# A decode kernel that streams 119 MB of weights and cache: the first weight load through the plain DMA call, and 16 or 32 equal columns in tail products that had one

## The chip, the cores and the metric

The kernel runs on one core of one Trainium2 chip. The metric is device time of one execution, in microseconds (us). It is quoted as a median over executions. The profile is one execution of the same program under the hardware profiler; its span counts from the first to the last instruction and is 1.7 us shorter than the device time of that run (286.36 us and 284.7 us for the kernel before). All executions count as fast (none lies over 1.5% above the fastest of its kernel).

## The reference, cut to what matters

One token (one row of 640 numbers) passes through attention over a cached window of 4096 keys per head, then through a gated MLP.

```python
x = A_x                                            # [1, 1, 640]
# attention: 32 heads of 192, the last W = 4096 positions of the caches
q = (layernorm(x) @ wq)                            # wq [640, 6144]
p = softmax(q . k_cache[:, :, -W:, :] * 192**-0.5)
h = x + (p @ v_cache[:, :, -W:, :]) @ wo           # wo [6144, 640]
# gated MLP on one position; S = 1, so w_sp and b_sp are single numbers
z  = gelu(layernorm(h) @ w_in)                     # w_in [640, 1536]
z1, z2 = z[:768], layernorm(z[768:])
out = h + (z1 * (w_sp * z2 + b_sp)) @ w_out        # w_out [768, 640]
```

All tensors are bf16. Keys and values are 50 MB each, wq and wo 7.9 MB each, w_in and w_out 2.9 MB together. Each is read once.

## The kernel before: the parts that matter

All large loads are issued by SyncE on one DMA queue, in the order of use: wq, then keys and values of 16 pairs of heads with wo between them, then the last wo piece, w_in and w_out. A load is issued when a buffer is free. The helper `load` builds the DMA instruction by hand instead of calling `nc.sync.dma_start`.

```python
def load(out, in_):
    eng = nc.sync
    eng.add_instruction(mybir.InstDMACopy(
        name=nc.get_next_instruction_name(), mode="Copy", queue="qSPDynamicHW",
        ins=eng.lower_ap_dma(in_, for_custom_bir_dma=True),
        outs=eng.lower_ap_dma(out, for_custom_bir_dma=True)))

wq_v = A_wq.rearrange("(c p i) n -> c p (i n)", c=DC, i=4)   # per c: 32 rows of 48 KB

def dma_wq(i):
    t = kvp.tile([P, KVE], BF16, tag="kv", name="wq_t")
    for c in range(2 * i, min(2 * i + 2, DC)):
        load(t[:, (c % 2) * HD:(c % 2 + 1) * HD], wq_v[c])
    tiles[("wq", i)] = t
```

The tail starts with the last products of probabilities and values. The attention output `o` of the last four heads goes through wo as 30 products with the weights stationary and one moving column; the partial row sums of the earlier heads are folded in first.

```python
# project(), last q only
for i in range(RQ):                                # RQ = 6
    for nb in range(DC):                           # DC = 5
        nc.tensor.matmul(attn_ps[:, nb:nb + 1], lhsT=wo_t[:, i * D + nb * P:i * D + (nb + 1) * P],
                         rhs=o[:, i:i + 1], start=False, stop=...)
...                                                # h, its sums, LayerNorm (cut)
def half_in(f0):
    zv = bank()
    for c in range(DC):
        for fb in range(FHC):                      # FHC = 6: 30 products a call
            nc.tensor.matmul(zv[:, fb:fb + 1], lhsT=w_in_sb[:, c, f0 + fb * P:f0 + (fb + 1) * P],
                             rhs=hb1[:, c:c + 1], start=..., stop=...)
    return zv[:, 0:FHC]

z2_ps = half_in(Fh)                                # gelu, second LayerNorm (cut)
z1_ps = half_in(0)                                 # gelu, gate (cut)
for c in range(FHC):
    for g in range(NG):                            # NG = 4, one group of columns of the array each
        nc.tensor.matmul(orow[32 * g:32 * g + 1, :], lhsT=gv[:, c:c + 1],
                         rhs=w_out_sb[:, c, g * OW:(g + 1) * OW], start=False, stop=(c == FHC - 1))
```

## Time and profile before

| | before |
|---|---|
| median of the first 3 executions | 286.6 us (286.29 to 286.65) |
| first weight packet starts | 2.07 us |
| 16 or more weight and cache packets in flight | 265.0 us |
| last w_out packet ends | 280.95 us |
| granted TensorE clock, mean | 0.803 |

The rows on packets are read from the trace's packet records.

The page of the kernel before. PE stands for TensorE's products, PEld for its weight loads, DVE for VectorE, ACT for ScalarE and POOL for GpSimd. In each row of digits a digit is a slice of 1/40 of the span in tenths; PEclk is the granted TensorE clock (the share of full clock that a throttle lets the engine have), DMA the mean busy share of the 16 engines.

```profile
span 284.7 us, 3101 instructions
PE 167.1 (59%) x1110; PEld 65.3 (23%) x1110; DVE 218.4 (77%) x288; ACT 75.2 (26%) x380; POOL 2.3 (1%) x10
...
PEclk9999979796598557955799558955797797999785
DMA  8999999999998999999999999999999999999993
GB/s 332 435 435 408 435 429 402 444 463 435 435 435 382 435 442 443 427 464 424 414 442 421 443 428 439 407 457 428 410 435 456 442 442 383 435 435 425 401 406 141
```

The DMA engines are the resource that is busy from end to end. VectorE comes next, at 77% of the span and 91% between 36 and 214 us, and the DMA engines stay busy there too (431 GB/s). The Trainium skill, "DMA: Bandwidth & Descriptors", section "Where 436 GB/s comes from", puts the ceiling of the core's SBUF ports at 435 GB/s; many slices here read 435 (some more, because a packet is booked whole at its start), and the mean is 420. So the kernel is within 4% of that ceiling, and, as far as this goes, only what lies before the first packet and after the last landings can go.

Busy time in two short stretches at the start of the kernel before. The columns are the stretch, its length, the busy time of PE, PEld, DVE, ACT and POOL, the granted clock, the DMA share and GB/s. A packet is booked whole at its start, so the DMA share can exceed 1.

```profile
1.60:2.00 0.40, 0.00 (x0) 0.00 (x0) 0.12 (x1) 0.40 (x1) 0.40 (x2) 1.00 0.01 3
2.00:2.40 0.40, 0.19 (x5) 0.19 (x5) 0.37 (x4) 0.22 (x2) 0.40 (x1) 1.00 4.25 1352
```

Nothing but the 1.2 KB of x moves before 2.0 us.

The tail on the timeline of the kernel before. Columns: start, duration, engine, line, operation, tile, and in brackets the idle time before it with what ended it.

```profile
273.26 0.51 PE L478 MATMUL attn_ps<-o_1888,wo_t 128*128 128x1 bf16 x15 [0.32 <-DVE o_1888 L464]
274.08 0.53 PE L478 MATMUL attn_ps<-o_1888,wo_t 128*128 128x1 bf16 x15 [0.30 <-DMA wo_t<-in_A_wo_dram]
...
274.96 0.48 PE L578 MATMUL sm_ps<-sums_1922,avgD_f 128*128 128x1 f32 x2 [0.36 <-DVE h_pc L574]
...
275.78 1.22 PE L589 MATMUL sm_ps<-hb_1930,w_in_sb 128*128 128x1 bf16 x30
...
279.16 0.96 PE L589 MATMUL sm_ps<-hb_1930,w_in_sb 128*128 128x1 bf16 x30
...
280.51 0.17 DVE L623 TENSOR_TENSOR gv<-z_2038,gz 128x6 bf16<-128x6 f32 x1
...
280.73 0.97 PE L626 MATMUL sc_ps<-w_out_sb,gv 128*1 128x160 bf16 x24 [0.61 <-DVE gv L623]
```

The second half of the last wo products waited for its weights. In the chain of work that ended last (start, length, what), that DMA is the link before the tail:

```profile
260.22 13.82 DMA wo_t<-in_A_wo_dram
...
274.08 0.54 PE attn_ps L478 x15
```

Busy time by stretch of the kernel before, columns as above. Read the third number from the right, the granted clock.

```profile
264.00:268.00 4.00, 3.59 (x38) 1.61 (x39) 0.61 (x4) 2.20 (x4) 0.00 (x0) 0.61 0.93 396
268.00:272.00 4.00, 3.44 (x92) 2.44 (x86) 2.89 (x4) 0.48 (x1) 0.00 (x0) 0.97 0.99 400
272.00:276.00 4.00, 2.62 (x59) 2.27 (x56) 0.98 (x6) 0.51 (x3) 0.00 (x0) 0.89 1.05 400
276.00:280.00 4.00, 3.51 (x75) 2.83 (x72) 2.49 (x14) 1.01 (x4) 0.00 (x0) 0.50 0.96 372
```

The clock record has two values only, 1.0 and 0.5, which agrees with the Trainium skill, "TensorE: Matmul & The Clock Gate", section "Part 1: The HAM clock gate", which says that the ratio is binary. It falls to 0.5 at 275.10 us and stays there to the end.

### The profile page before, as it was taken

How to read it: one execution, taken by the hardware profiler on the slowest of the kernel's cores; microseconds unless marked ns; L12 is line 12 of the kernel's file. 1: busy time of each engine (PE TensorE's matmuls, PEld its weight loads, DVE VectorE, ACT ScalarE, POOL GpSimd, SP SyncE). 2: the span in 40 equal slices, each digit the busy share in tenths (PEclk: the TensorE clock that was granted, in tenths of full speed). 3: DMA queues.
4: the chain of work that ended last, by engine and by line, in shares of the span. 5: the costliest groups of instructions: out<-in, count | busy, mean ns of one | idle time of the engine just before them, and what ended most of it. 6: DMA issues, size and time to landing. Idle time of an engine off the chain costs nothing.

```text
span 284.7 us, 3101 instructions
## 1 busy us (share of the span) xinstructions
PE 167.1 (59%) x1110; PEld 65.3 (23%) x1110; DVE 218.4 (77%) x288; ACT 75.2 (26%) x380; POOL 2.3 (1%) x10
## 2 busy tenths in 40 slices
PE   0329935773755377725852585536971767764774
PEld 0103412221211022211220121112320222321463
DVE  7300099889999999998499999996699949995443
ACT  2001247413274431122344440143101010202301
POOL 3000000000000000000000000000000000000000
PEclk9999979796598557955799558955797797999785
DMA  8999999999998999999999999999999999999993
GB/s 332 435 435 408 435 429 402 444 463 435 435 435 382 435 442 443 427 464 424 414 442 421 443 428 439 407 457 428 410 435 456 442 442 383 435 435 425 401 406 141
DMA packets 5404, 119.53 MB, mean 420 GB/s; under 512 B 973, under 2 KB 2254, under 8 KB 2830
## 3 DMA queue, kind: packets, MB, share of 16 engines
q1 hardware_dynamic: 5384, 119.35, 97.8%
q8 instruction: 8, 0.13, 0.2%
q14 instruction: 6, 0.05, 0.0%
q10 hardware_dynamic: 6, 0.00, 0.0%
HBM read 119.34 MB, written 0.00 MB: 419 GB/s over the span
## 4 chain that ended last, share of the span: by engine, by line
DMA 42%; DVE 41%; PE 13%; issue 2%; SPq 1%; ACT 0%; DVEq 0%; ACTq 0%
DVE k_t L316 22%; DMA k_t<-in_A_k_cache_dram 21%; DMA v_t<-in_A_v_cache_dram 9%; DMA wq_t<-in_A_wq_dram 7%; DMA wo_t<-in_A_wo_dram 5%; PE sc_ps L264 5%; DVE S L309 5%; DVE ob L437 4%; DVE S L330 4%; PE sc_ps L323 3%; PE pv_174 L412 1%; PE attn_ps L473 1%; SPq L58 1%; PE sm_ps L340 1%; DVE gm L342 1%
## 5 line engine op out<-in xcount | busy, mean ns | idle before, releaser
L316 DVE TENSOR_TENSOR k_t<-k_t,q_205 128x6144 bf16<-128x6144 bf16 x32 | 107.1, 3351 | 13.1 <-DMA k_t<-in_A_k_cache_dram 13.1
L323 PE MATMUL sc_ps<-k_t,ident_bf 128*128 128x512 bf16 x282 | 87.1, 468 | 50.6 <-DVE k_t L316 50.6
L306 ACT ACTIVATE k_t<-k_t 128x192 bf16<-128x192 bf16 x144 | 49.9, 347 | 32.8 <-DVE k_t L316 32.8
L323 PEld LDWEIGHTS <-ident_bf 128*128 128x128 bf16 x282 | 30.6, 113 | 98.3 <-issue 63.9
L306 ACT ACTIVATION_READ_ACCUMULATOR k_t<-k_t 128x1 f32 x144 | 26.8, 186 | 0.0
L309 DVE TENSOR_REDUCE S<-k_t 128x16 f32<-128x3072 bf16 x8 | 26.8, 3345 | 0.0
L264 PE MATMUL sc_ps<-wq_t,xn_126 128*128 128x512 bf16 x60 | 17.4, 449 | 10.4 <-DMA wq_t<-in_A_wq_dram 8.1
L330 DVE TENSOR_REDUCE S<-sc_ps 128x16 f32<-128x512 f32 (+1 forms) x32 | 21.8, 682 | 0.5 <-PE sc_ps L323 0.5
L273 DVE TENSOR_SCALAR sp_f<-sm_ps 128x1 f32<-128x1 f32 x3 | 0.3, 153 | 25.3 <-PE sm_ps L270 25.3
L359 ACT ACTIVATE E_125<-S,bias 128x64 bf16<-128x64 f32 x10 | 3.5, 360 | 48.1 <-DVE bias L349 48.1
L359 ACT ACTIVATE E_123<-S,bias 128x64 bf16<-128x64 f32 x12 | 4.2, 360 | 41.9 <-DVE bias L349 41.9
L359 ACT ACTIVATE E_124<-S,bias 128x64 bf16<-128x64 f32 x10 | 3.5, 361 | 37.9 <-DVE bias L349 37.9
L266 ACT ACTIVATE q_205<-sc_ps 128x512 bf16<-128x512 f32 x6 | 3.6, 597 | 30.1 <-PE sc_ps L264 30.1
L264 PEld LDWEIGHTS <-xn_126 128*128 128x128 bf16 x60 | 6.5, 109 | 20.9 <-issue 13.6
L412 PE MATMUL pv_174<-v_t,E_124 128*8 128x512 bf16 (+1 forms) x72 | 8.9, 521 | 2.0 <-DMA v_t<-in_A_v_cache_dram 2.0
L342 DVE TENSOR_REDUCE gm<-sm_ps 2x1 f32<-2x128 f32 x16 | 4.5, 278 | 7.1 <-PE sm_ps L340 7.1
L412 PE MATMUL pv_172<-v_t,E_125 128*8 128x512 bf16 (+1 forms) x72 | 7.5, 472 | 3.1 <-DMA v_t<-in_A_v_cache_dram 3.1
L412 PE MATMUL pv_174<-v_t,E_123 128*8 128x512 bf16 (+1 forms) x48 | 5.8, 521 | 1.0 <-DMA v_t<-in_A_v_cache_dram 1.0
L412 PE MATMUL pv_172<-v_t,E_123 128*8 128x512 bf16 (+1 forms) x72 | 6.2, 424 | 0.0
L412 PE MATMUL pv_174<-v_t,E_125 128*8 128x512 bf16 (+1 forms) x48 | 5.0, 474 | 1.6 <-DMA v_t<-in_A_v_cache_dram 1.6
L412 PEld LDWEIGHTS <-E_125 128*8 128x8 bf16 (+1 forms) x120 | 3.5, 87 | 9.3 <-issue 7.2
L412 PEld LDWEIGHTS <-E_124 128*8 128x8 bf16 (+1 forms) x120 | 3.6, 89 | 8.3 <-issue 6.4
(237 smaller groups left out, 148.3 us busy)
## 6 DMA issues: line engine op xcount, KB each, us to landing
k_t<-in_A_k_cache_dram SPq DMA_DIRECT2D x15, 3072.0 KB, 29.8
v_t<-in_A_v_cache_dram SPq DMA_DIRECT2D x15, 3072.0 KB, 29.6
wq_t<-in_A_wq_dram SPq DMA_DIRECT2D x5, 1536.0 KB, 11.2
wo_t<-in_A_wo_dram SPq DMA_DIRECT2D x7, 960.0 KB, 19.9
k_t<-in_A_k_cache_dram SPq DMA_DIRECT2D x2, 1536.0 KB
v_t<-in_A_v_cache_dram SPq DMA_DIRECT2D x1, 1536.0 KB
w_in_sb<-in_B_w_in_dram SPq DMA_DIRECT2D x2, 576.0 KB, 14.6
wo_t<-in_A_wo_dram SPq DMA_DIRECT2D x2, 480.0 KB, 13.8
```

What stands on the lines that cost most here:

```text
L58: eng.add_instruction(mybir.InstDMACopy(name=nc.get_next_instruction_name(), mode="Copy", queue="qSPDynamicHW", ins=eng.lower_ap_dma(in_, ...
L264: nc.tensor.matmul(psv, lhsT=xn2[:, c, a, :], rhs=wc[:, gq:gq + 4, a, w0:w0 + P], start=(c == 0 and a == 0), stop=(c == DC - 1 and a == 1))
L266: nc.scalar.activation(out=q2f[:, gq:gq + 4, w0:w0 + P], in_=psv, func=ACT.Copy, scale=scale / 16)
L306: nc.scalar.activation(out=k3[:, j, :], in_=k3[:, j, :], func=ACT.Copy, accum_out=S[:, j:j + 1])
L309: nc.vector.tensor_reduce(out=st[t]["S"][:, J - JS:J], in_=products(t)[:, J - JS:J, :], axis=AX.X, op=ALU.add)
L316: nc.vector.tensor_tensor(out=kc, in0=kc, in1=q2[:, t:t + 1, :].to_broadcast([P, JC, Dh]), op=ALU.mult)
L323: nc.tensor.matmul(psv, lhsT=ident_bf[:], rhs=products(t)[:, j0:j1, n * g:(n + 1) * g], start=(n == 0), stop=(n == Dh // g - 1))
L330: nc.vector.tensor_reduce(out=S[:, j0:j1], in_=st[t]["ps"][ch], axis=AX.X, op=ALU.add)
L342: nc.vector.tensor_reduce(out=gm[:], in_=mT[0:2, 0:P], axis=AX.X, op=ALU.max)
L359: nc.scalar.activation(out=E[:, :, a], in_=S[:], func=ACT.Exp, bias=bias[:, a:a + 1], accum_out=zq[q][:, a, b:b + 1])
L412: nc.tensor.matmul(pv[p0:p0 + 2 * n, :].rearrange("p (k r i) -> p k r i", k=n, r=32), lhsT=E[:, j0:j0 + n, :].rearrange("p j a -> p (j a)" ...
L437: nc.vector.tensor_reduce(out=ob[:, i0:i0 + ni], in_=flat.rearrange("p (k r i) -> p i r k", k=n, i=ni), axis=AX.X, op=ALU.add)
```

## The change

Two independent parts. The first issues the first wq load with the plain call `nc.sync.dma_start` and gives it rows of 12 KB instead of 48 KB. The second streams 16 equal columns through the last wo products (a power of two that still fits beside the row sums in the bank), and 32 through the w_in products; the readers take column 0. The results are the same numbers. Its likely purpose is to keep TensorE busier at no cost.

```diff
     def dma_wq(i):
         t = kvp.tile([P, KVE], BF16, tag="kv", name="wq_t")
         for c in range(2 * i, min(2 * i + 2, DC)):
-            load(t[:, (c % 2) * HD:(c % 2 + 1) * HD], wq_v[c])
+            dst = t[:, (c % 2) * HD:(c % 2 + 1) * HD]
+            if c == 0:
+                nc.sync.dma_start(out=dst, in_=A_wq[0:P])
+            else:
+                load(dst, wq_v[c])
 ...
-    rows = attn_ps[:, DC + 3:DC + 3 + CUT[1]]
+    AW = 16
+    attn = attn_ps[:, 0:(DC + 1) * AW].rearrange("p (c w) -> p c w", w=AW)
+    rows = attn_ps[:, (DC + 1) * AW:(DC + 1) * AW + CUT[1]]
 ...
-                    nc.tensor.matmul(attn_ps[:, nb:nb + 1], lhsT=wo_t[...],
-                                     rhs=o[:, i:i + 1], start=False,
+                    nc.tensor.matmul(attn[:, nb, :], lhsT=wo_t[...],
+                                     rhs=o[:, i:i + 1].to_broadcast([P, AW]), start=False,
 ...                                 # fold(): 2 x 16 columns likewise
+    ZW = 32
     def half_in(f0):
-        zv = bank()
+        zv = bank()[:, 0:FHC * ZW].rearrange("p (f w) -> p f w", w=ZW)
 ...
-                nc.tensor.matmul(zv[:, fb:fb + 1], lhsT=w_in_sb[...], rhs=hb1[:, c:c + 1],
+                nc.tensor.matmul(zv[:, fb, :], lhsT=w_in_sb[...],
+                                 rhs=hb1[:, c:c + 1].to_broadcast([P, ZW]),
 ...
-        return zv[:, 0:FHC]
+        return zv[:, :, 0]
```

No load and no product is added or moved.

More of the change, by code (lines that the diff above doesn't have):

```diff
@@ L276 @@
     CUT = (0, 3 * P, D)
-    rows = attn_ps[:, DC + 3:DC + 3 + CUT[1]]
+    AW = 16
+    attn = attn_ps[:, 0:(DC + 1) * AW].rearrange("p (c w) -> p c w", w=AW)
+    rows = attn_ps[:, (DC + 1) * AW:(DC + 1) * AW + CUT[1]]
     nc.vector.memset(rows, 0.0)
-    nc.vector.memset(attn_ps[:, DC:DC + 1], (eps * DC) ** 0.5)
+    nc.vector.memset(attn[:, DC, :], (eps * DC) ** 0.5)
     obq = {}
@@ L477, in project @@
                 for nb in range(DC):
-                    nc.tensor.matmul(attn_ps[:, nb:nb + 1], lhsT=wo_t[:, i * D + nb * P:i * D + (nb + 1) * P],
-                                     rhs=o[:, i:i + 1], start=False,
+                    nc.tensor.matmul(attn[:, nb, :], lhsT=wo_t[:, i * D + nb * P:i * D + (nb + 1) * P],
+                                     rhs=o[:, i:i + 1].to_broadcast([P, AW]), start=False,
                                      stop=(q == NQ - 1 and i == RQ - 1 and nb == DC - 1))
@@ L486, in fold @@
             w = 2 if c + n < DC else 1
-            nc.tensor.matmul(attn_ps[:, c:c + n * (w - 1) + 1:n], lhsT=rows_sb[:, c * P:(c + 1) * P], rhs=halfsel[:, 0:w],
+            nc.tensor.matmul(attn[:, c:c + n * (w - 1) + 1:n, :], lhsT=rows_sb[:, c * P:(c + 1) * P], rhs=halfsel[:, 0:w, None].to_broadcast([P, w, AW]),
                              start=(c == 0), stop=False)
@@ L573 @@
     sums2 = [const.tile([P, 1], F32, name=f"sums2{k_}") for k_ in range(2)]
-    nc.vector.tensor_scalar(out=h_pc[:], in0=attn_ps[:, 0:DC], scalar1=1.0, scalar2=0.0, op0=ALU.mult, op1=ALU.add,
+    nc.vector.tensor_scalar(out=h_pc[:], in0=attn[:, 0:DC, 0], scalar1=1.0, scalar2=0.0, op0=ALU.mult, op1=ALU.add,
                             accum_out=sums2[0][:])
-    nc.scalar.activation(out=hsq[:], in_=attn_ps[:, 0:DC + 1], func=ACT.Square, accum_out=sums2[1][:])
+    nc.scalar.activation(out=hsq[:], in_=attn[:, :, 0], func=ACT.Square, accum_out=sums2[1][:])
     mean_ps = bank()[:, 0:1]
@@ L583 @@
     rstd2 = ln_rstd16(neg_var(mean_ps, square_ps))
+    ZW = 32
     def half_in(f0):
-        zv = bank()
+        zv = bank()[:, 0:FHC * ZW].rearrange("p (f w) -> p f w", w=ZW)
         for c in range(DC):
             for fb in range(FHC):
-                nc.tensor.matmul(zv[:, fb:fb + 1], lhsT=w_in_sb[:, c, f0 + fb * P:f0 + (fb + 1) * P], rhs=hb1[:, c:c + 1],
+                nc.tensor.matmul(zv[:, fb, :], lhsT=w_in_sb[:, c, f0 + fb * P:f0 + (fb + 1) * P],
+                                 rhs=hb1[:, c:c + 1].to_broadcast([P, ZW]),
                                  start=(c == 0 and fb == 0), stop=(c == DC - 1 and fb == FHC - 1))
-        return zv[:, 0:FHC]
+        return zv[:, :, 0]
     z2_ps = half_in(Fh)
```

## The prediction

> **What bounds the kernel now.** The DMA stream, end to end. The page's DMA row stands at 9 from the second slice to the last but one, 119.5 MB at a mean of 420 GB/s over a span of 284.7 us. The packet records show all 16 DMA engines busy at once for 255.6 us and never fewer than ten between 2.7 us, soon after the first weight packet (2.07 us), and 279.6 us; the last w_out packet ends at 280.95 us. VectorE (77%) and TensorE (59%) have slack. So only two pieces can shrink: the 2.07 us before the stream, and the tail after the last weights.
>
> **The tail** (timeline, from 274 us). The last wo half lands at 274.08; 15 products; LayerNorm sums; 30 w_in products (18 from 275.78, the other 12 held by their DMA until 276.53); gelu at 277.39, released by VectorE's rstd chain, not by the products; 30 more products 279.16 to 280.12; VectorE's gz ends 280.40, level with gelu z1 at 280.42; w_out products 280.73 to about 281.7; store; end.
>
> **What the change does.**
> 1. First wq load. SyncE issues it at 0.74 us and takes 0.55 us; its first packet starts 0.78 us later. The change gives it the plain call that the x and spatial loads use: their later ScalarE issues took 0.22 and 0.27 us (the first 0.50). Estimate: 0.2 to 0.3 us saved, and as the DMA engines never go idle, all later landings move earlier by about that. Against it: 12 KB rows for 48 KB. A 12 KB packet takes 461 ns, a 48 KB one 1815, so 8 against 2 cost 58 ns per engine. Net estimate: 0.2 us.
> 2. 16 columns (wo). One-column pairs are spaced 25 ns at full clock. The Trainium skill, "TensorE: Matmul & The Clock Gate", section "Back-to-back issue gap", gives 1 to 64 columns one floor, about 25 ns; the trace agrees at one column. 16 columns should be free.
> 3. 32 columns (w_in). These run at granted clock 0.5 (from 275.45 us), spaced 26 to 27 ns. 512-column products at full clock follow every 213 ns with their weight load hidden, so a 32-column stream (estimate 26.7 ns at half clock, by scaling) should also hide it. Cost: about 26 ns more for the last of each 30.
> 4. Strided PSUM reads, wider memset, wider fold: under 20 ns on the path.
>
> The likely purpose of 2 and 3 is to show the clock throttle a busier TensorE. If full clock came back in the tail, the w_out products (133 ns apart per group of four at half clock) and the LayerNorm matmuls would save an estimated 0.3 to 0.5 us. I doubt it: before each return to 1.0 the trace has a window of nearly unbroken 512-column work, and 30 x 32 columns fill only 0.8 of 3.4 us.
>
> **Sum.** Minus 0.2 us (load), plus 0.05 us (columns), minus 0.1 us for the chance of a better clock: 286.35 us, 80% range 285.7 to 286.9. Chances: faster by over 2% 0.01, within 2% 0.98, slower 0.01.
>
> **What would show it.** First issue at or under 0.35 us and first packet by 1.85 us; last w_out packet and wo landing earlier by about 0.2 us; wo spacing 25 ns; w_in spacing 26 to 28 ns; granted clock still 0.5 from about 275 us; time from wo landing to the end unchanged within 0.1 us.
>
> **What would make it wrong.** If weight loads do not overlap short moving streams, w_in spacing becomes about 53 ns and the second 30 cost 0.8 us on the path. If the throttle stays open, up to 0.5 us is won, of which the last w_out landing caps part. If the first load's latency, not its issue, sets the first packet, step 1 gives nothing.

Three slips in it: the clock fell at 275.10 us in the profile's time, not at 275.45. Its 255.6 us is the time with exactly 16 large packets in flight; 16 or more were in flight for 265.0 us. And the 512-column products at full clock mostly follow every 215 to 216 ns, not 213. None of them changes its argument.

## The result, and the profile after

The changed kernel takes 286.14 us (median of 6, 286.11 to 286.40) beside 286.55 us for the kernel before (median of 6 executions). The ratio is 0.9987, with a 95% interval of 0.9974 to 1.0000. Ratios here are the mean time of one kernel's fast runs over that of the other's from the same rounds, so they are not quite the ratio of the quoted medians. The prediction of 286.35 us, range 285.7 to 286.9, holds.

| | before | after | difference |
|---|---|---|---|
| first issue of SyncE | 0.55 us | 0.38 us | -0.17 |
| first weight packet starts | 2.07 us | 1.75 us | -0.32 |
| last packet of the last wo piece ends | 273.68 us | 273.32 us | -0.36 |
| h starts on VectorE | 274.74 us | 274.42 us | -0.32 |
| its LayerNorm result hb starts | 275.49 us | 275.27 us | -0.22 |
| gate product gv starts | 280.51 us | 280.28 us | -0.23 |
| last w_out packet ends | 280.95 us | 280.59 us | -0.36 |
| span | 284.66 us | 284.45 us | -0.21 |

The page after:

```profile
span 284.5 us, 3101 instructions
PE 170.5 (60%) x1110; PEld 66.5 (23%) x1110; DVE 218.3 (77%) x288; ACT 75.2 (26%) x380; POOL 2.3 (1%) x10
...
PEclk9999996889599757995687557957896679979575
DMA  8999999999998999999999999999999999999993
```

The start of the changed kernel, stretches as before:

```profile
1.60:2.00 0.40, 0.00 (x0) 0.00 (x0) 0.12 (x1) 0.40 (x1) 0.40 (x2) 1.00 1.65 276
2.00:2.40 0.40, 0.00 (x0) 0.00 (x0) 0.36 (x4) 0.22 (x2) 0.40 (x1) 1.00 0.00 0
```

Nine engines now start before 2.0 us; in between none starts, and the other seven start by 2.65 us (before: eleven by 2.32 and five by 2.90). The tail on the timeline after:

```profile
273.23 1.05 PE L484 MATMUL attn_ps<-o_1888,wo_t 128*128 128x16 bf16 x30 [0.32 <-DVE o_1888 L470]
...
274.64 0.59 PE L584 MATMUL sm_ps<-sums_1922,avgD_f 128*128 128x1 f32 x2 [0.36 <-DVE h_pc L580]
...
275.56 1.07 PE L597 MATMUL sm_ps<-hb_1930,w_in_sb 128*128 128x32 bf16 x30
...
278.94 0.98 PE L597 MATMUL sm_ps<-hb_1930,w_in_sb 128*128 128x32 bf16 x30
...
280.28 0.17 DVE L632 TENSOR_TENSOR gv<-z_2038,gz 128x6 bf16<-128x6 f32 x1
...
280.50 0.97 PE L635 MATMUL sc_ps<-w_out_sb,gv 128*1 128x160 bf16 x24 [0.59 <-DVE gv L632]
```

There are two readings. The second thirty of w_in take 0.98 us with 32 columns and took 0.96 us with one: the columns are free, as forecast. And the first float32 product for the LayerNorm (L584, before L578) takes 0.59 us where it took 0.48: the 0.32 us won at the start has become 0.22 by then. The cause is the clock:

```profile
264.00:268.00 4.00, 3.96 (x38) 1.68 (x39) 0.51 (x3) 1.99 (x4) 0.00 (x0) 0.50 0.96 408
268.00:272.00 4.00, 4.00 (x92) 2.70 (x86) 2.92 (x4) 0.48 (x1) 0.00 (x0) 0.76 0.98 399
272.00:276.00 4.00, 2.91 (x65) 2.65 (x64) 1.18 (x6) 0.51 (x3) 0.00 (x0) 0.67 1.05 400
276.00:280.00 4.00, 3.40 (x68) 2.64 (x64) 2.39 (x14) 1.06 (x5) 0.00 (x0) 0.50 0.93 362
```

In this execution the clock fell at 273.36 us, before those products, and in the kernel before at 275.10, after them. The same skill section says that the activity window runs free of the program. The traces agree: within each profile all changes of the clock lie whole multiples of about 3.41 us apart (here 252.88, 256.30, 263.12, 269.95 and 273.36 us), and the place of this grid differs from execution to execution. Over the profiles without fillers (below) and with an unshifted start, the last fall lies anywhere from 273.36 to 276.58 us. load_only with one column and all_wq with 16 and 32, whose grids happen to lie within 0.06 us of each other, have the same last fall (274.65 and 274.71 us). So this 0.1 us is most likely a draw of one execution and not a cost of the change.

The clock was also at 0.5 from 263.12 to 269.95 us, through most of the last value products. In the profile after, the view of the chain that ended last therefore names TensorE's value products instead of the wo DMA.

```profile
234.08 29.92 DMA v_t<-in_A_v_cache_dram
...
264.04 1.87 PE pv_172 L418 x12
...
269.15 1.54 PE pv_174 L408 x29
...
273.23 1.06 PE attn_ps L484 x30
```

This view leaves out short waits, and here that misleads. The wo products started at 273.23 us, at nearly the same time as before. But the first of the second fifteen started at 273.72 us, 0.05 us after its weights' landing (273.67 us by the semaphore record) and 0.11 us after the product before it, where the first fifteen follow each other every 25 to 30 ns. In the kernel before it started at 274.08 us, also 0.05 us after the landing (274.03), and 0.46 us after the product before it. So the wo load was still last in both. Its 0.36 us came through, less the 0.04 us by which the second fifteen were slower at half clock: h starts 0.32 us earlier. What shrank is the wait for it, from 0.44 to 0.09 us. In after_again (below) nothing was left of it: the second fifteen followed after 29 ns.

That the two are so close was not in the prediction at all. At the end of the stream the DMA and the TensorE chain of the last value products arrive nearly together, and the clock decides which is last.

### The profile page after: what moved, and what is told of

Its sections match the earlier page's. It is cut to its first block, busy times and chain, and to the rows that moved or that the text cites. A ratio compares the mean times of both kernels' runs of the same rounds, so it can differ in the third digit from the quotient of the medians.

```text
span 284.5 us, 3101 instructions
## 1 busy us (share of the span) xinstructions
PE 170.5 (60%) x1110; PEld 66.5 (23%) x1110; DVE 218.3 (77%) x288; ACT 75.2 (26%) x380; POOL 2.3 (1%) x10
## 4 chain that ended last, share of the span: by engine, by line
DVE 38%; DMA 37%; PE 21%; issue 2%; SPq 1%; ACT 0%; DVEq 0%; ACTq 0%
DMA k_t<-in_A_k_cache_dram 20%; DVE k_t L322 20%; DMA v_t<-in_A_v_cache_dram 11%; PE sc_ps L329 8%; DMA wq_t<-in_A_wq_dram 6%; PE sc_ps L268 5%; DVE S L315 5%; DVE ob L443 4%; DVE S L336 3%; PE attn_ps L479 2%; PE pv_172 L418 1%; PE sm_ps L346 1%; PE pv_174 L418 1%; DVE gm L348 1%; SPq L58 1%
## 5 line engine op out<-in xcount | busy, mean ns | idle before, releaser
L329 PE MATMUL sc_ps<-k_t,ident_bf 128*128 128x512 bf16 x282 | 89.2, 477 | 48.0 <-DVE k_t L322 48.0
L268 PE MATMUL sc_ps<-wq_t,xn_126 128*128 128x512 bf16 x60 | 18.3, 469 | 10.1 <-DMA wq_t<-in_A_wq_dram 7.9
```

The costliest lines, as they stand in the source:

```text
L268: nc.tensor.matmul(psv, lhsT=xn2[:, c, a, :], rhs=wc[:, gq:gq + 4, a, w0:w0 + P], start=(c == 0 and a == 0), stop=(c == DC - 1 and a == 1))
L329: nc.tensor.matmul(psv, lhsT=ident_bf[:], rhs=products(t)[:, j0:j1, n * g:(n + 1) * g], start=(n == 0), stop=(n == Dh // g - 1))
```

## The experiments

Theory A: the gain is the earlier start of the weight stream, passed through whole, since the DMA engines never run dry; the columns do nothing. Rivals: B, the columns give it, through the products or the clock; and within A, that the smaller rows and not the issue path start the engines earlier. Each call ran on one chip and shares 11 executions of the kernel before; its median differs by up to 0.4 us from call to call, so compare within a call. An execution over 287 us of a kernel that mostly stays under it is called a stray below. All twelve runs gave correct results.

### First call: one part at a time, the row form, and a late start

**load_only**: the kernel before with the first-load hunk of the diff alone.

> Only the first wq load is changed (plain call, 12 KB rows); the tail products keep one column. Theory A (the gain is the earlier start of the weight stream, passed through whole): ratio to before about 0.9987, first weight packet at about 1.75 us, last w_out packet end near 280.6 us, time about 0.3 to 0.4 us under before. Theory B (the wider columns give the gain, through the clock or the products): ratio 1.000. Theory C (both give half): about 0.9993.

Measured: 286.18 us (285.95 to 286.35, 5 runs), before 286.48 us (11 runs). Ratio 0.9984, interval 0.9967 to 1.0001. First issue 0.39 us, first weight packet at 1.75 us:

```profile
1.60:2.00 0.40, 0.00 (x0) 0.00 (x0) 0.12 (x1) 0.40 (x1) 0.40 (x2) 1.00 1.13 246
```

The load alone gives the whole 0.30 us in the median. The last w_out packet ended at 280.79 us where 280.6 was expected; the landing of the last packets differs by 0.2 us from run to run.

**cols_only** and **cols_again**: the changed kernel with the first-load hunk undone. Run twice.

```diff
-            dst = t[:, (c % 2) * HD:(c % 2 + 1) * HD]
-            if c == 0:
-                nc.sync.dma_start(out=dst, in_=A_wq[0:P])
-            else:
-                load(dst, wq_v[c])
+            load(t[:, (c % 2) * HD:(c % 2 + 1) * HD], wq_v[c])
```

> Only the 16 and 32 columns; the first wq load is as before. Theory A: ratio 1.000 (up to 0.05 us slower), first weight packet at about 2.07 us, w_in products still 26 to 27 ns apart, granted clock 0.5 from some point between 272 and 276 us to the end. Theory B: ratio about 0.9987. Theory C: 0.9993.

Measured: 287.16 us (286.37 to 288.32, 6 runs), ratio 1.0018, interval 0.9994 to 1.0041. Three of the six lie at 286.37, 286.41 and 286.85, the other three at 287.48 to 288.32. One of the eleven executions of the kernel before on that chip was such a stray too (287.89). First packet as before the change:

```profile
1.60:2.00 0.40, 0.00 (x0) 0.00 (x0) 0.12 (x1) 0.40 (x1) 0.40 (x2) 1.00 0.01 3
```

This is no gain, but the three strays left it open whether the columns harm. So it was run again, beside the changed kernel, in the second call.

> The same kernel as cols_only, again, because three of its six times lay over 287 us against one of eleven of the kernel before. If the wider columns do harm: again several times over 287, ratio about 1.002. If those were stray executions (of the kind that the kernel before also shows once, at 287.89): median 286.4 to 286.6, ratio 1.000 within 0.0005.

Measured in the second call: 286.80 us (286.64 to 286.85, 6 runs, no stray), before 286.74 us. Ratio 0.9989, interval 0.9971 to 1.0007; it is under 1 only because four of the eleven executions of the kernel before were strays (287.45 to 288.25). Without those four the kernel before has a median of 286.67 us, 0.13 under this one. So the columns neither gain nor, in these twelve executions, do harm that repeats. A cost of about 0.1 us is not excluded.

**rows_only**: one column, the first load issued by hand as before, but with rows of 12 KB.

```diff
-            load(t[:, (c % 2) * HD:(c % 2 + 1) * HD], wq_v[c])
+            dst = t[:, (c % 2) * HD:(c % 2 + 1) * HD]
+            load(dst, A_wq[0:P] if c == 0 else wq_v[c])
```

> One column, and the first wq load in 12 KB rows but issued the old way. It parts the row form from the issue path. Theory A1 (the shorter issue starts the stream earlier): issue 0.55 us, first packet at 2.0 to 2.1 us, ratio 1.000 to 1.0002. Theory A2 (the smaller rows start the engines earlier, whatever the issue path): first packet before 1.9 us, ratio about 0.9987.

Measured: 286.60 us (286.41 to 286.96, 5 runs), ratio 0.9998, interval 0.9979 to 1.0018. The issue took 0.58 us and the first packet started at 2.09 us. The row form alone starts nothing earlier; the issue path does. (The plain call with 48 KB rows was not tried.) It also shows that the path does more than shorten the issue: the plain call's first packet starts 0.64 us after the end of its issue (1.11 to 1.75 us), the hand-built one's 0.78 us after (1.29 to 2.07).

This run bears on another point by the way: what a faster clock in the tail is worth. Here the clock stayed open until 276.58 us, and gv started at 280.37 us, 0.14 us earlier than in the kernel before. Yet the w_out products ended at 281.70 us as there, because they took 1.11 us instead of 0.97:

```profile
280.59 1.11 PE L630 MATMUL sc_ps<-w_out_sb,gv 128*1 128x160 bf16 x24 [0.61 <-DVE gv L627]
```

In the instruction records the last group of four started 0.32 us after the one before it instead of 0.13, and 0.04 us after the landing of the last w_out load (281.36 us by the semaphore record). So the last landing caps what a faster tail can win. From that landing to VectorE's reading of the products it took 0.45 us in the kernel before (281.30 to 281.75) and 0.59 us in the changed kernel (280.94 to 281.53). With the clock fully open (warm_tail, below) it took 0.33 us. So full clock in the tail was worth some 0.12 us before and 0.25 us after the change, by estimate from these three profiles.

**late_start**: the changed kernel with four small loads ahead of the first weight load.

```diff
+    junk = const.tile([1, 4, 64], BF16)
+    for k_ in range(4):
+        nc.sync.dma_start(out=junk[:, k_, :], in_=A_x[0, :, 64 * k_:64 * k_ + 64])
+
     def dma_wq(i):
```

> The changed kernel with four small loads of x (128 bytes each, into a scratch that nobody reads) issued on SyncE ahead of the first wq load; each should take about 0.25 to 0.35 us of issue. Theory A: the first weight packet moves by 1.0 to 1.4 us against the changed kernel and the time follows one to one, so about 287.1 to 287.5 us, ratio to before 1.002 to 1.0035. Rival (a late start is made up somewhere in 280 us of stream, since VectorE and buffers set part of the pace): under half of the shift arrives, ratio under 1.001.

Measured: 287.68 us (287.53 to 288.59, 5 runs), ratio 1.0041, interval 1.0022 to 1.0061: slower, with the interval clear of 1. The first weight packet started at 2.94 us, 1.19 us later than in the changed kernel, and the last w_out packet ended at 281.86 us, 1.27 us later. Against load_only on the same chip, which has one column, the median rose by 1.50 us. So a shift of the start arrives at the end at least in full. About 0.3 us more than the shift is left open: the columns differ, the four loads also use up completion semaphores, and the issue of the third wq load took 1.00 us against 0.93.

### Second call: repeat, double the columns, hold the clock

**after_again**: the changed kernel once more.

> The changed kernel beside cols_again on one chip. Theory A (earlier start): 0.3 to 0.4 us under before, ratio 0.9986, and lower than cols_again by the same. If the columns harm: no gain over before.

Measured: 286.50 us (286.48 to 287.98, 6 runs, one stray), ratio 0.9988, interval 0.9965 to 1.0011. The median is 0.30 us under cols_again, which differs by the first load alone, and 0.24 under before (0.17 without the four strays of before). The size of the gain, 0.2 to 0.4 us, repeats on each chip where it was tried; each single ratio has an interval that just reaches 1.

**cols64**: the suspected cost of the columns, doubled.

```diff
-    ZW = 32
+    ZW = 64
```

> The changed kernel with 64 instead of 32 equal columns in the w_in products: the suspected cost doubled. At granted clock 0.5 the products should follow each other every 53 ns instead of 26 to 27 ns (64 columns at 1.2 per ns), so the second thirty takes 1.6 us instead of 0.8. That thirty is level with VectorE's gz chain, so the time should rise by 0.6 to 0.8 us, to about 286.9. It would show that 32 columns were free because the stream is just as long as the weight load beneath it. Rival (the floor is per instruction, and 64 columns are also free): spacing under 30 ns, time unchanged. If the granted clock returns to 1.0 in the tail through the added columns, spacing 27 ns and the time falls.

Measured: 287.37 us (286.75 to 288.22, 6 runs), ratio 1.0014, interval 0.9991 to 1.0037; 0.87 us over after_again in the median, where 0.6 to 0.8 was expected. Products follow each other every 53 to 54 ns. The timeline has the two thirties:

```profile
275.78 1.76 PE L597 MATMUL sm_ps<-hb,w_in_sb 128*128 128x64 bf16 x30
...
279.35 1.78 PE L597 MATMUL sm_ps<-hb,w_in_sb 128*128 128x64 bf16 x30
```

1.78 us where 32 columns took 0.98: 32 columns were free at the 0.5 clock only because their stream (32 columns at 1.2 per ns, 26.7 ns; 512-column products follow every 427 ns at this clock) is no longer than the 26 to 27 ns that one column already took. The Trainium skill, "TensorE: Matmul & The Clock Gate", section "Back-to-back issue gap", lists 1 to 64 columns as one cost at full clock; at the 0.5 clock the trace does not allow that reading, and the same section's cold formula (columns over 1.2 per ns) gives the 53 ns that were measured. The granted clock in the tail stayed at 0.5 even with 64 columns.

**warm_tail**: seven products of 512 columns that nobody reads, where TensorE waits in the tail, into a PSUM bank that is free by then.

```diff
+    def filler(bank_, n):
+        for _ in range(n):
+            nc.tensor.matmul(bank_[:], lhsT=ident_bf[:], rhs=q2[:].rearrange("p a b -> p (a b)")[:, 0:512],
+                             start=True, stop=True)
 ...
     values(NP - 1, vt, LAST[-2], J)
+    filler(pv_tiles[0], 1)
     scaled(NP - 1)
     columns(oT, NQ - 1, 1)
+    filler(pv_tiles[0], 1)
     project(NQ - 1, oT)              # and one filler between its two halves
+    filler(pv_tiles[0], 1)
 ...
     h_rows(0, NG // 2)
+    filler(pv_tiles[0], 1)
 ...
     z1_ps = half_in(0)
+    filler(pv_tiles[0], 2)
```

> The changed kernel with seven products of 512 columns that nobody reads, put where TensorE waits in the last 12 us (one after the last value products, one before and one in the middle of and one after the last wo products, one before the second LayerNorm's sums, two after the last w_in products). It asks whether the throttle can be held open in the tail and what that is worth. If the activity suffices: granted clock 1.0 to the end, w_out groups 67 ns apart instead of 133, time 0.2 to 0.4 us under the changed kernel. If not: the fillers run at 427 ns each and delay the chain, clock 0.5 as before, time 0.1 to 0.5 us over the changed kernel. I think the second the likelier.

Measured: 286.31 us (285.99 to 286.56, 6 runs, no stray), ratio 0.9973, interval 0.9952 to 0.9993, and 0.19 us under after_again in the median. The likelier-seeming outcome was wrong: in the profiled execution the clock stayed open from 271.20 us to the end. The grid of its clock changes lies within 0.1 us of those of load_only, cols64 and all_wq, whose clocks fell at 274.65 to 274.71 us, so the grid's place is not what kept it open. But the work also came later there (see below), so one profile does not put it down to the fillers alone.

```profile
272.00:276.00 4.00, 3.46 (x80) 2.47 (x81) 0.69 (x5) 0.51 (x3) 0.00 (x0) 1.00 1.05 399
276.00:280.00 4.00, 3.15 (x81) 2.70 (x83) 2.63 (x15) 1.02 (x5) 0.00 (x0) 1.00 0.96 372
```

From the first wo product to the start of the last w_out product it took 7.41 us, against 7.90 in the changed kernel's profile and 8.10 before. The timeline has where it came from, and what caps it:

```profile
275.54 0.38 PE L594 MATMUL sm_ps<-sums,avgD_f 128*128 128x1 f32 x2
...
280.87 0.83 PE L647 MATMUL sc_ps<-w_out_sb,gv 128*1 128x160 bf16 x24 [0.47 <-DVE gv L644]
```

The LayerNorm product takes 0.38 us instead of 0.59. The w_out groups of four follow each other every 68 to 70 ns instead of 133, but the last group started only 0.32 us after the one before it: it needs the last landing of the stream (281.42 us, as in rows_only). In this execution the value stage had been cold as well (0.55 in 264 to 268 us, 0.60 in 268 to 272) and the first wo product started at 274.06 us, 0.83 us later than in the profile after.

### Third call: are the columns worth something then, and where do the strays come from

**warm_onecol**: warm_tail with one column.

```diff
-    AW = 16
+    AW = 1
 ...
-    ZW = 32
+    ZW = 1
```

> warm_tail with the wide columns taken back to one (the fillers and the early load stay). It asks whether the columns do anything for the clock once there is other work: in warm_tail the 60 w_in products of 32 columns are some 1900 of the columns streamed after 275 us. If they matter: the clock falls to 0.5 again somewhere from 274 to 279 us (w_in products 26 to 27 ns apart in the second thirty, w_out groups 120 to 133 ns), time 0.1 to 0.3 us over warm_tail. If the fillers alone do it: clock 1.0 to the end, time as warm_tail within 0.1 us.

Measured: 286.74 us (286.15 to 287.67, 6 runs, three of them at 287.00 or over), ratio 0.9984, interval 0.9958 to 1.0010. In the profile the clock fell to 0.5 at 275.56 us and stayed there. That is what was expected if the columns matter, but the window in which it fell began 1 us later than the one in warm_tail, and the run was a stray, so one profile each does not settle it. What the columns do for the clock stays open.

The stray is of use for itself. Busy time and chain of this execution, 287.67 us:

```profile
264.00:268.00 4.00, 2.97 (x34) 1.49 (x35) 1.98 (x5) 2.19 (x4) 0.00 (x0) 0.67 0.90 386
268.00:272.00 4.00, 4.00 (x67) 2.51 (x59) 2.92 (x4) 0.48 (x1) 0.00 (x0) 0.50 1.00 405
```

```profile
269.40 2.12 PE pv L408 x25
271.53 1.07 PE attn_ps L495 x6
...
274.37 0.51 PE attn_ps L486 x15
```

TensorE was busy for the whole of 268 to 272 us at the 0.5 clock, and the wo products started at 274.37 us (0.32 us of it a filler), where they started at 273.26 and 273.23 us in the profiles before and after. The weights had long landed (last packet 273.56 us). The one other profile of an execution well above its kernel's others, late_start's 288.59 us (the other four at 287.53 to 287.73), has no filler and shows the same: clock 0.50 in 268 to 272 us, and the first wo product 1.02 us after the last wo packet (275.61 and 274.59 us), where the changed kernel's profile has it 0.09 us ahead of that packet. A cold start of the stage is not enough: after_again and cols_again were at 0.5 from 263.8 to 270.7 us and took 286.52 and 286.85 us. In the two strays the half clock lasted to 272.15 and 273.55 us.

**warm_both**: warm_tail and six more fillers near 262 us, where TensorE waited some 2 us for value data.

```diff
     scaled(NP - 3)
     vt = tiles.pop(("v", NP - 2))
+    filler(pv_tiles[1], 6)
     values(NP - 2, vt, 0, J // 2)
```

> warm_tail with six more unread products of 512 columns where TensorE waits some 2 us for value data near 262 us. The idea under test: executions 1 to 1.7 us over the rest (4 of 11 of the kernel before in the last call, at mean clocks of 0.78 to 0.81) are those in which the clock stays at 0.5 through the last value products, so that they end after the wo data has landed. If so: the clock is at 1.0 from before 268 us on, no execution over 287, and a spread of under 0.5 us, median as warm_tail or 0.1 to 0.2 us lower. If the stray executions come from elsewhere (the DMA, say), they stay.

Measured: 286.72 us (286.62 to 286.88, 6 runs), ratio 0.9983, interval 0.9959 to 1.0008. No stray, where five of the eleven executions of the kernel before on that chip were strays (287.57 to 288.30). The value stage is now warm:

```profile
264.00:268.00 4.00, 3.80 (x62) 1.86 (x63) 2.31 (x6) 2.21 (x5) 0.00 (x0) 1.00 0.94 400
268.00:272.00 4.00, 2.58 (x80) 2.00 (x70) 2.41 (x5) 0.47 (x1) 0.00 (x0) 1.00 0.99 403
272.00:276.00 4.00, 3.69 (x56) 2.66 (x57) 0.88 (x6) 0.51 (x3) 0.00 (x0) 0.50 1.05 401
```

But now TensorE waited from 268.6 us for the last value pieces, and the clock fell at 272.02 us; the tail was cold, the median no better than the good executions of before (286.71 us without the strays).

**all_wq**: all five wq loads as plain calls in 12 KB rows, beside the changed kernel's columns.

```diff
-            dst = ...
-            if c == 0:
-                nc.sync.dma_start(out=dst, in_=A_wq[0:P])
-            else:
-                load(dst, wq_v[c])
+            nc.sync.dma_start(out=t[:, (c % 2) * HD:(c % 2 + 1) * HD], in_=A_wq[c * P:(c + 1) * P])
```

> The changed kernel with all five wq loads as plain calls in 12 KB rows. Theory A says that only the first issue lies on the path, since the DMA engines are never idle after it; the other four only cost 58 ns per engine and load (8 packets of 460 ns against 2 of 1815): last w_out packet 0.1 to 0.3 us later than in the changed kernel, time 0.1 to 0.3 us over it, so 0.1 to 0.2 us under before. Rival (each shorter issue gains): another 0.2 us or more under the changed kernel.

Measured: 286.99 us (286.26 to 287.95, 6 runs, two strays), ratio 0.9994, interval 0.9967 to 1.0021. The later issues took 0.41 to 0.68 us instead of 0.54 to 0.93, and nothing came of it; the last w_out packet ended at 281.01 us, 0.18 and 0.27 later than in the two other profiles of the call with one plain load (280.83 and 280.74). That is the size of the expected packet cost, but the time itself is too noisy to say more than that there is no further gain.

### Fourth call: both gaps filled

**warm_more**: warm_both with three more fillers at the wait near 268.6 us.

```diff
-    values(NP - 1, vt, 0, LAST[-3])
+    values(NP - 1, vt, 0, LAST[1])
+    filler(pv_tiles[0], 3)
+    values(NP - 1, vt, LAST[1], LAST[-3])
```

> warm_both with three more unread 512-column products in the 1.3 us for which TensorE waited near 268.6 us for the last value pieces, since the clock there fell to 0.5 at 272.0 us. The hope: clock 1.0 from about 264 us to the end, no execution over 287, and 0.4 to 0.7 us under the median of before (ratio 0.997 to 0.9985 in its fast runs, lower where before has strays). If the fillers come late (after a cold stretch they take 427 ns each), the last value products are delayed and it is no better than warm_tail, about 0.3 us under before.

Measured: 286.32 us (286.25 to 286.61, 6 runs), before 286.82 us (11 runs, four at 287.34 to 288.09). Ratio 0.9974, interval 0.9954 to 0.9994. No stray again. The clock fell later than in warm_both, at 274.35 us, not "never":

```profile
268.00:272.00 4.00, 3.53 (x86) 2.37 (x85) 1.83 (x3) 0.00 (x0) 0.00 (x0) 1.00 0.97 396
272.00:276.00 4.00, 3.88 (x60) 2.46 (x58) 0.94 (x6) 0.50 (x3) 0.00 (x0) 0.79 1.05 400
```

With warm_tail this is the best version found: both beat the kernel before with an interval clear of 1, by 0.26 to 0.27%. In the means warm_more gains some 0.7 us; the early start, about 0.3 us, is less than half of it, and the strays of the kernel before (four of eleven, each about 1 us long) are of the size of the rest, by estimate from these numbers.

## Why the prediction was right, point by point

- **The stream bounds the kernel and a shift of its start arrives whole: right.** In the profiles -0.32 us at the first packet became -0.36 at the last. late_start moved the start by 1.19 us and the time by at least as much.
- **The load term was mis-sized: -0.2 us net predicted, about -0.3 measured** (load_only -0.30 in the median; the changed kernel -0.41, and -0.24 on another chip). The estimate took its 0.2 to 0.3 us from ScalarE's tiny issues of 0.22 and 0.27 us; the issue of a 1.5 MB load fell by only 0.17 us, to 0.38, over the 0.35 forecast. What was missed is that the wait from the end of the issue to the first packet fell as well, by 0.14 us (0.78 to 0.64). rows_only shows that both belong to the path, not to the rows. The predicted packet cost of 0.06 us is too small for these runs to see.
- **Free columns: right.** Spacing 26 to 27 ns in the w_in products as predicted. The wo products kept 25 ns for the six that started before the clock fell, and 26 to 27 after. cols_again and cols64 agree with the reason given. The 0.05 us set aside for their cost is not resolved.
- **The throttle stays shut for the changed kernel: right,** at 0.5 from 273.36 us on, and so the 0.1 us credited for the chance of a better clock did not come. Nor was there as much to win: the prediction put full clock in the tail at 0.3 to 0.5 us, of which the last w_out landing would cap part. By the landing times (see rows_only) it caps more than was thought, leaving by estimate 0.12 us in the kernel before and 0.25 us in the changed one. The reason given, that a full window of dense work is needed, is too strict for staying open: warm_tail held the clock through 274.61 to 278.03 us with 58 products and 2,356 moving columns.
- **Tail unchanged within 0.1 us: missed by little.** From the last wo packet to the end of the span it took 11.13 us after and 10.98 before; the clock's earlier fall explains nearly all of the difference (0.04 us in the second fifteen wo products, 0.10 us in the LayerNorm products).
- **What was not foreseen:** the last value products are nearly as late as the stream, and their clock decides about 1 us of single executions. In the last four calls 14 of 44 executions of the kernel before are strays over 287 us, at a mean clock of 0.786; the other 30 have 0.806. Fillers in the wait before that stage removed them (0 of 12 in warm_both and warm_more, 9 of 22 of the kernel before in the same calls). That a value stage cold to its end makes the strays is supported by this and by the two that were profiled, and not proven: the unprofiled ones have no clock record by time, and warm_tail and cols_again, without fillers before that stage, had no stray in six executions each either.

So the sum came out right with two errors of 0.1 us that partly offset: the load gained more than predicted, and nothing came from the clock. The range of 285.7 to 286.9 us would have held for no change at all (286.55 us) too, so it is the packet times and the separate runs, not the total, that bear the prediction out.

## What to carry to other kernels

In a kernel whose DMA engines never run dry, the time to the first packet is worth its full length and the issues behind it are worth nothing: put the cheapest issue path on the first large load alone. Extra columns in a product are free only up to the spacing that one column has anyway, 25 to 27 ns here, and how many columns that is depends on the granted clock. Before you trust a 0.1% difference, look at the spread of single executions: here a free-running clock window moved some of them by over 1 us, and in the two runs that filled the waits in front of the last chain no such execution was seen. And before you credit a faster tail, look up when the last load lands.

## What the Trainium skill lacked or had wrong

- "TensorE: Matmul & The Clock Gate", section "Part 1: The HAM clock gate", says the clock goes cold after at least one idle window of about 3.4 us. Here it fell after windows that were not idle: at 275.10 us in the kernel before, at the end of a step of the 3.41 us grid in which 52 products with 1,580 moving columns started; at 275.56 us in warm_onecol, after 75 products with 4,664 columns (3,072 of them in value products that used two columns of the array). It stayed open in warm_tail after a step with 58 products and 2,356 columns. So what shuts the clock here is neither a whole idle window nor the count of columns alone, and the page gives no threshold for it.
- The same page, section "Back-to-back issue gap": its table of one cost for 1 to 64 columns is for full clock. At the 0.5 clock 1 and 32 columns were spaced 26 to 27 ns and 64 columns 53 ns. The section gives no floor of its own for the 0.5 clock.
- No page tells that the plain DMA call and a hand-built one differ in issue: 0.38 against 0.55 us for the same 1.5 MB load, and 1.02 against 1.33 us from the start of the issue to the first packet. "DMA: Bandwidth & Descriptors", section "Specifications", gives about 0.6 us to the first byte for this kind of queue; that fits only the stretch after the end of the issue (0.64 and 0.78 us).
- "DMA: Bandwidth & Descriptors", section "Where 436 GB/s comes from", says that for loads from HBM the HBM side (about 358 GB/s) binds. Taken alone, that sentence does not fit one core that streams by itself: the mean here was 420 GB/s over the span. The same section says that 358 is one core's half of what two share and puts a 16 MB load at 425 GB/s, which fits. That the ports and not something else bind at 420 is shown by no run.
- No page tells that the 16 engines do not start together on a first load: nine started from 1.75 to 1.95 us and seven from 2.49 to 2.65 us in the changed kernel. The split differs from run to run (eight by 1.83 us in load_only).
